# A scheduled attention and FFN kernel: more room behind each wait in the order, measured lengths in the planner, and small softmax steps moved

## The chip, the cores and the metric

The kernel runs on one core of a Trainium2 chip. The metric is the device time of one execution in microseconds. PE is the matrix engine (TensorE), PEld its weight loads, ACT is ScalarE, DVE is VectorE, POOL is GpSimd, and SP is the engine that issues the DMA transfers. Each of them runs its own instructions in the order in which they were written, and waits for semaphores of the others.

## The reference, cut to what matters

```python
def mab(q, kv):                       # scale = 1/sqrt(128)
    s = scale * (q @ kv.T)
    a = exp(s - s.max(-1));  a /= a.sum(-1) + 1e-09
    return a @ kv
h = mab(I, x)                         # x: 4 x 12480 x 128, I: 32 x 128
y = mab(x, h)                         # 4 x 12480 x 128
out = relu(y @ w_in) ** 2 @ w_out     # w_in: 128 x 2048, w_out: 2048 x 128
```

All is float32. The first attention has 32 queries over all tokens of a batch; the second has each token as a query over 32 keys.

## The kernel before, in words

A batch is cut into 13 units of 960 tokens, so there are 52 units, and a unit is two blocks of 480 tokens. After a start-up (the first attention of batch 0, and the weights), units run one after the other. For each unit PE does the FFN: 32 products named `h` of 480 columns (line 755) give relu inputs in PSUM, and 96 products named `op` (line 795) multiply the squared relus by `w_out`. Two `h` products fill one of two PSUM buffers, called a pair here: `h_4_0_2` is pair 2 of block 0 of unit 4 (order rows leave the batch out, and end in a running number). ACT empties a pair with a relu (line 763, into `g`), and after two pairs it squares `g` in place (line 774). DVE rounds `g` to `hi` (line 778) and takes the rest `lo` = `g` - `hi` (line 782); PE multiplies `hi` by two parts of `w_out` and `lo` by one. The buffers: two for `h`, three for `g`, two for `hi`, two for `lo`.

Beside this FFN stream every unit carries small work for later units: transposes of x (`xtp`, copied to `xt`), the two attentions' scores (`na`) and mixes (`nb`), and the second attention's softmax: a maximum, the difference `d`, its exponential on ACT, the rounded part `sk` and its rest, the sum `z`, and three small steps on 120x8 elements (lines 637, 640, 644: add 1e-9, invert, square) that give `zz`. `zz` scales the output when a block is turned back (`otp`, line 823, into `osb`). `ot` is the copy of a finished `op` sum out of PSUM, and `sw` that of the attention weights, which DMAs then spread into `st`, the input of `h`. In batch 3 there is no first attention left to do, so its units carry less.

The order on every engine comes from a list scheduler, class `Plan`, when the program is built. A task has an engine (or two to choose from, `"ACT|DVE"`), a length in ns, a due time, and tasks that it needs. `offer` sets when it is ready: the latest end of what it needs, plus a latency by the engine that it waits for. `room_at` adds 60 ns after the last user of a buffer. At each step `run` takes for each engine the task that can start first, by due time among those ready at once, and of these the earliest. `port` keeps GpSimd tasks and some VectorE tasks from overlapping in the plan. The chip then runs the orders as written, whatever times the plan had in mind.

Of the kernel before, what the change touches and what calls it, by code (L numbers as in the profile page):

```python
# [21 lines left out]
TS = 120  # L22
# [5 lines left out]
class Task:  # L28
    def __init__(self, engine, ns, fn, due, needs, port, mode, takes, order):
        self.engine, self.ns, self.fn, self.due = engine, ns, fn, due  # L30
        self.needs, self.port, self.mode, self.takes, self.order = needs, port, mode, takes, order
        self.start = self.end = self.ready = None
        self.waiting = 0
        self.then = []
# [9 lines left out]
class Plan:  # L44
# [7 lines left out]
    LATENCY = {"PE": 220.0, "ACT": 150.0, "DVE": 150.0, "POOL": 150.0, "SP": 2500.0}  # L52
    SWITCH = 95.0

    def __init__(self, room):
        self.room, self.tasks = room, []

    def add(self, engine, ns, fn, due, needs=(), port=False, mode=None, takes=(), reads=()):

        t = Task(engine.split("|"), ns, fn, due, [n for n in needs if n is not None], port, mode, takes, len(self.tasks))  # L60
        for b in list(takes) + list(reads):
            b.users.append(t)
        self.tasks.append(t)
        return t

    def run(self):
# [20 lines left out]
        def room_at(t):  # L87
            at = 0.0
            n = {}
            for b in t.takes:  # L90
                n[b.tag] = n.get(b.tag, 0) + 1
                old = taken.get(b.tag, [])
                i = len(old) + n[b.tag] - 1 - self.room[b.tag]
                if i >= 0:
                    for u in (old[i].users if i < len(old) else ()):
                        if u.end is None:
                            return None
                        at = max(at, u.end + 60.0)
            return at
# [42 lines left out]
def induced_attention_then_squared_relu_ffn(  # L142
# [22 lines left out]
    XT, OT, ST, SKH = ("ACT|DVE", "ACT|DVE"), ("ACT|DVE", "ACT|DVE"), "ACT|DVE", "ACT|DVE"  # L165
# [11 lines left out]
    plan = Plan(dict(xn=3, early=6, xt=NU + 1, m=2, h=2, o=2, g=GB, hi=HB, lo=LB, st=2, sw=2, words=2))  # L177
# [57 lines left out]
    def weights(name, load, use, due):  # L235
# [54 lines left out]
        t = add("SP", 2100, words, due - 6000, takes=[buf])  # L290
# [65 lines left out]
    class First:  # L356
        def __init__(self, b, u, due, early=False):

            self.b, self.u, self.early, self.n = b, u, early, f"{b}_{u}"
            self.s = s = state.setdefault(b, {"xt": {}, "chain": None, "bxt": {}})  # L360
            self.bx = Buffer("early" if early else "xn")
            self.bt = s["bxt"][u] = Buffer("xt")
            lead = 2500 if early else 8000

            def load():
                self.xn = (pools["early"] if early else xn_pool).tile(
                    [TS, NT, C], F32, tag="xn", name=f"xn_{self.n}"
                )
                nc.sync.dma_start(self.xn, x_v[b, :, u * NT:(u + 1) * NT, :])

            loaded = add("SP", 2000, load, due - lead - (4000 if early else 20000), takes=[self.bx])
            self.turned = []
            for k in range(2):
                self.turned.append(self.turn(k, due - lead + k * lead * 0.4, loaded))

        def turn(self, k, due, loaded):
# [18 lines left out]
            t = add("PE", 420, turn, due, [loaded] + self.turned,  # L395
# [194 lines left out]
    class Second:  # L590
# [13 lines left out]
        def weigh(self, scored, where, bank_, due, step):  # L604
# [31 lines left out]
            def norm1():  # L636
                nc.vector.tensor_scalar_add(v["z"], v["z"], 1e-9)

            def norm2():
                nc.vector.reciprocal(v["z"], v["z"])  # L640

            def norm3():
                s["zz", u] = tiny.tile([TS, G, 1], F32, tag="zz", name=f"zz_{n}")
                nc.vector.tensor_mul(s["zz", u], v["z"], v["z"])


            def high():
                v["sk"] = att.tile([TS, Q, 2, 2, M], F32R, tag="sk", name=f"sk_{n}")
                copy(th, v["sk"][:, :, :, 0, :], v["d"].rearrange("t (k q) m -> t q k m", q=Q))
# [39 lines left out]
            th = add(SKH, (300, 250), high, d + 3 * step, [tp], port=True)  # L689
# [44 lines left out]
    def ffn_block(b, u, k, second, t0, first_needs):  # L734
# [7 lines left out]
        def quad(j, last):  # L742
# [4 lines left out]
            for i in range(2):  # L747
# [19 lines left out]
                t = add("PE", 217, lambda wide=wide: wide(0), d, need, takes=[bh], reads=[second.bst])  # L767
                w.setdefault("begun", t)
                t = add("PE", 217, lambda wide=wide: wide(1), d, [t], reads=[bh, second.bst])
                relus.append(add("ACT", 855, relu, d + 1000, [t] + first_needs + relus,  # L770
# [13 lines left out]
            sq = add("ACT", 1696, square, due + 4000, relus, reads=[bg])  # L784
            th = add("DVE", 1070, high, due + 5700, [sq], port=True, takes=[bhi], reads=[bg])
            tl = add("DVE", 2076, low, due + 7800, [th], port=True, takes=[blo], reads=[bg, bhi])
            for m, (wo, name, from_, buf) in enumerate((
                (wo_hi, "hi", th, bhi), (wo_lo, "hi", th, bhi), (wo_hi, "lo", tl, blo),
            )):
                for i in range(2):  # L790
# [10 lines left out]
                    last = add("PE", 434, products, due + 8000 + 600 * (2 * m + i), [from_, last, w_outs[j]],  # L801
# [32 lines left out]
        td = add(OT[k], (455, 570), done, end + 1000, [last], reads=[bo])  # L834
# [77 lines left out]
```

## Time and profile before

| | us |
|---|---|
| median of three runs (lowest to highest) | 1776.12 (1775.27 to 1777.15) |
| the profiled execution's own time | 1777.57 |
| its span, first to last instruction | 1775.8 |
| busy: PE / PEld / ACT / DVE / POOL | 1736.6 / 1415.7 / 1652.7 / 1641.0 / 22.2 |

The profiled execution is one run, taken by the hardware profiler; its time is 1.8 us above its span and 1.45 us above the median. Busy is the union of an engine's instructions. A matmul's record is longer than the step to the next one, since they overlap: 480 columns are 0.38 us in a record and 0.22 us from start to start. So PE reads as busy even where it lost time, and its losses are seen in the starts.

### The profile page before, as it was taken

What the parts mean: (1) busy time and instruction counts of PE and PEld (TensorE: products, weight loads), DVE (VectorE), ACT (ScalarE), POOL (GpSimd) and SP (SyncE); (2) the same over time, 40 slices, a digit from 0 to 9 for tenths busy, and PEclk for the clock granted to TensorE, in tenths of its full rate; (3) what the DMA queues carried; (4) which work ended last, traced back from release to release, by engine and by line L of the source; (5) the groups of instructions that cost most, each with busy time, mean ns of one, the idle gap of its engine ahead of it and who ended that gap; (6) DMA issues with size and microseconds to landing.
All of it is one profiled execution on the core that took longest, in us unless ns stands there. A gap on an engine that the chain in (4) does not pass through costs nothing.

```text
span 1775.8 us, 24582 instructions
## 1 busy us (share of the span) xinstructions
PE 1736.6 (98%) x9625; PEld 1415.7 (80%) x9625; DVE 1641.0 (92%) x1736; ACT 1652.7 (93%) x1765; POOL 22.2 (1%) x22
## 2 busy tenths in 40 slices
PE   7799999999999999999999999999999999999998
PEld 4488888888788888888888888888887788888886
DVE  6799999999999999999999999999999998999988
ACT  6699999999999999999999999999999999999997
POOL 1200000000000000000000000000000000000000
PEclk9899999999999999999999999999999999999999
DMA  9211211211121211211211211111101001010110
GB/s 234 62 45 45 56 34 45 56 35 44 34 56 45 56 37 43 56 45 36 59 29 45 56 45 38 52 46 48 31 23 42 26 23 45 23 45 23 35 33 23
DMA packets 33532, 82.48 MB, mean 46 GB/s; under 512 B 5032, under 2 KB 20424, under 8 KB 33416
## 3 DMA queue, kind: packets, MB, share of 16 engines
q1 hardware_dynamic: 33416, 80.91, 17.4%
q8 instruction: 76, 1.25, 0.3%
q14 instruction: 40, 0.33, 0.1%
HBM read 29.77 MB, written 25.56 MB: 31 GB/s over the span
## 4 chain that ended last, share of the span: by engine, by line
PE 67%; ACT 20%; issue 9%; DVE 2%; DMA 1%; SPq 0%; ACTq 0%; DVEq 0%
PE op L795 43%; PE h L755 15%; ACT g L763 13%; ACT g L774 6%; PE otp L815 2%; PE xtp L388 1%; PE ap L660 1%; PE na L599 1%; DMA xn<-in_x_dram 1%; PE wp L559 1%; PE s2t L616 1%; PE na L403 1%; DVE lo L782 1%; PE ep L437 1%; ACT xt L224 1%
## 5 line engine op out<-in xcount | busy, mean ns | idle before, releaser
L782 DVE TENSOR_TENSOR lo<-g,hi 128x1920 fp32r<-128x1920 f32 x416 | 895.6, 2153 | 13.0 <-DVE hi L778 0.9
L763 ACT ACTIVATE g<-h 128x960 f32<-128x960 f32 x832 | 783.0, 982 | 47.8 <-PE h L755 42.1
L774 ACT ACTIVATE g<-g 128x1920 f32<-128x1920 f32 x416 | 759.4, 1826 | 5.1
L755 PE MATMUL h<-st,hw 128*128 128x480 f32 x1664 | 644.3, 388 | 15.4 <-ACT g L763 12.5
L778 DVE CAST hi<-g 128x1920 fp32r<-128x1920 f32 x416 | 480.1, 1154 | 78.8 <-ACT g L774 75.3
L795 PE MATMUL op<-lo,wo_hi 128*128 128x480 f32 x1664 | 511.1, 389 | 0.3 <-DVE lo L782 0.3
L795 PE MATMUL op<-hi,wo_lo 128*128 128x480 f32 x1664 | 506.0, 390 | 0.0
L795 PE MATMUL op<-hi,wo_hi 128*128 128x480 f32 x1664 | 481.8, 382 | 0.2 <-DVE hi L778 0.2
L755 PEld LDWEIGHTS h<-st,hw 128*128 128x128 f32 x1664 | 314.3, 189 | 108.3 <-ACT g L763 55.7
L795 PEld LDWEIGHTS op<-hi,wo_hi 128*128 128x128 f32 x1664 | 311.4, 188 | 50.3 <-DVE hi L778 0.9
L795 PEld LDWEIGHTS op<-hi,wo_lo 128*128 128x128 f32 x1664 | 299.6, 188 | 50.6 <-issue 11.7
L795 PEld LDWEIGHTS op<-lo,wo_hi 128*128 128x128 f32 x1664 | 302.2, 189 | 40.4 <-issue 2.7
L224 ACT COPY ot<-op 128x480 f32<-128x480 f32 x99 | 55.8, 564 | 27.1 <-PE op L795 26.9
L823 DVE TENSOR_TENSOR osb<-otp,zz 120x512 f32<-120x512 f32 x104 | 71.2, 684 | 4.2 <-PE otp L815 2.5
L388 PE MATMUL xtp<-ident,xn 120*128 120x120 f32 x416 | 62.7, 278 | 7.3 <-DMA xn<-in_x_dram 5.4
L388 PEld LDWEIGHTS xtp<-ident,xn 120*128 120x128 f32 x416 | 51.0, 147 | 21.0 <-issue 6.2
L815 PE MATMUL otp<-ident,ot 128*120 128x128 f32 x416 | 62.4, 272 | 0.6 <-ACT ot L224 0.6
L815 PEld LDWEIGHTS otp<-ident,ot 128*120 128x120 f32 x416 | 48.9, 137 | 15.6 <-ACT ot L224 6.6
L224 ACT COPY xt<-xtp 128x480 f32<-128x480 f32 x66 | 36.3, 555 | 13.7 <-PE xtp L388 13.6
L660 PEld LDWEIGHTS ap<-identr,sk 120*128 120x128 f32 x208 | 31.5, 193 | 4.8 <-DVE hw L568 1.5
L599 PE MATMUL na<-xt,hT 128*32 128x240 f32 x416 | 32.3, 382 | 0.0
L660 PE MATMUL ap<-identr,sk 120*128 120x120 f32 x208 | 29.5, 265 | 0.0
(95 smaller groups left out, 673.9 us busy)
## 6 DMA issues: line engine op xcount, KB each, us to landing
xn<-in_x_dram SPq DMA_DIRECT2D x52, 480.0 KB, 4.3
st<-sw SPq DMA_DIRECT2D x208, 120.0 KB, 2.6
out_dram<-osb SPq DMA_DIRECT2D x52, 480.0 KB, 3.5
words_i<-in_moe_w_in_dram SPq DMA_DIRECT2D x4, 512.0 KB, 10.3
words_o<-in_moe_w_out_dram SPq DMA_DIRECT2D x4, 512.0 KB, 7.5
ind_sb<-in_inducing_dram SPq DMA_DIRECT2D x1, 16.0 KB, 1.8
```

Of the source, the lines that this page charges most:

```text
L224: ENG[task.by](dst, src)
L388: nc.tensor.transpose(v["tp"][:, t * TS:(t + 1) * TS], self.xn[:, 4 * k + t, :], ident[:TS, :TS])
L599: nc.tensor.matmul(where[q * M:(q + 1) * M, :], self.s["hT"][:, :M], self.s["xt"][self.u][:, q * 2 * TS:(q + 1) * 2 * TS], start=True, sto ...
L660: nc.tensor.matmul(ap[:, q * TS:(q + 1) * TS], v["sk"][:, q].rearrange("t k a m -> t (k a m)"), identr[:TS, :TS], start=(q == 0), stop=(q ...
L755: nc.tensor.matmul(c["hp"][:, l, :BLK], s["hw"][:, f * P:(f + 1) * P], s["st", u][:, k, :], start=True, stop=True,)
L763: nc.scalar.activation(v["g"][:, 2 * i:2 * i + 2, :], c["hp"][:, :, :BLK], AF.Relu)
L774: nc.scalar.activation(v["g"], v["g"], AF.Square)
L778: nc.vector.tensor_copy(v["hi"], v["g"])
L782: nc.vector.tensor_sub(v["lo"], v["g"], v["hi"])
L795: nc.tensor.matmul(w["op"][:, :BLK], wo[:, 4 * j + l, :], v[name][:, l, :], start=(j == m == l == 0), stop=(j == NQ - 1 and m == 2 and l = ...
L815: nc.tensor.transpose(tp[:TS, q * P:(q + 1) * P], w["ot"][:, q * TS:(q + 1) * TS], ident)
L823: nc.vector.tensor_mul(s["osb", u].rearrange("t (q k) c -> t k q c", k=2)[:, k], w["tp"][:TS, :].rearrange("t (q c) -> t q c", q=Q), s["zz ...
```

## The change

The planner gets three edits. A task now has a margin `late`, added to the latency behind everything that it waits for: 200 ns for PE and 100 ns for the others in the main part, none in the start-up, and some set by hand. A PE task that waits for a PE task has no latency at all (before: 220 ns). A buffer is free 100 ns plus the margin after its last user (before: 60 ns). Some lengths and the latency behind DVE are new numbers. In the second attention the add of 1e-9 goes to GpSimd; then GpSimd squares, and DVE inverts the square; the copy to `sk` is always on DVE.

```diff
-    LATENCY = {"PE": 220.0, "ACT": 150.0, "DVE": 150.0, "POOL": 150.0, "SP": 2500.0}
+    LATENCY = {"PE": 220.0, "ACT": 150.0, "DVE": 185.0, "POOL": 150.0, "SP": 2500.0}
+    LATE = {"PE": 200.0, "other": 100.0}
...
+        if late is None:
+            late = self.LATE["PE" if engine == "PE" else "other"] if due > self.begin else 0.0
...
-            t.ready = max([n.end + self.LATENCY[n.by] for n in t.needs], default=0.0)
+            t.ready = 0.0
+            for n in t.needs:
+                own = n.by == "PE" and t.engine == ["PE"]
+                t.ready = max(t.ready, n.end + (0.0 if own else self.LATENCY[n.by] + t.late))
...
-                        at = max(at, u.end + 60.0)
+                        at = max(at, u.end + 100.0 + t.late)
...
+    LATE_G1, LATE_OT = 150.0, 400.0
...
             def norm1():
-                nc.vector.tensor_scalar_add(v["z"], v["z"], 1e-9)
+                nc.gpsimd.tensor_scalar(v["z"], v["z"], 1e-9, 0.0, ALU.add, ALU.add)
             def norm2():
-                nc.vector.reciprocal(v["z"], v["z"])
+                v["zz"] = tiny.tile([TS, G, 1], F32, tag="z3", name=f"z3_{n}")
+                nc.gpsimd.tensor_mul(v["zz"], v["z"], v["z"])
             def norm3():
                 s["zz", u] = tiny.tile([TS, G, 1], F32, tag="zz", name=f"zz_{n}")
-                nc.vector.tensor_mul(s["zz", u], v["z"], v["z"])
+                nc.vector.reciprocal(s["zz", u], v["zz"])
...
-            t = add("DVE", 75, norm1, d + 5 * step, [t])
-            t = add("DVE", 113, norm2, d + 5 * step, [t])
-            self.zz = add("DVE", 198, norm3, d + 5 * step, [t])
+            t = add("POOL", 150, norm1, d + 5 * step, [t])
+            t = add("POOL", 150, norm2, d + 5 * step, [t])
+            self.zz = add("DVE", 120, norm3, d + 6 * step, [t])
...
-                t = add("PE", 217, lambda wide=wide: wide(0), d, need, takes=[bh], reads=[second.bst])
+                t = add("PE", 219, lambda wide=wide: wide(0), d, need, takes=[bh], reads=[second.bst], late=LATE_G1)
...
-            sq = add("ACT", 1696, square, due + 4000, relus, reads=[bg])
-            th = add("DVE", 1070, high, due + 5700, [sq], port=True, takes=[bhi], reads=[bg])
+            sq = add("ACT", 1706, square, due + 4000, relus, reads=[bg], late=0)
+            th = add("DVE", 1070, high, due + 5700, [sq], port=True, late=200, takes=[bhi], reads=[bg])
...
-        td = add(OT[k], (455, 570), done, end + 1000, [last], reads=[bo])
+        td = add(OT[k], (455, 570), done, end + 1500, [last], reads=[bo], late=LATE_OT)
```

What that does to the orders is seen at three places. First PE in batch 1, where unit 4 begins. Before, the two halves of a pair stand apart, with `op` products between them, and ten products stand between the end of pair 2 and pair 4, which takes the same PSUM buffer:

```order
L755 MATMUL h_4_0_2_6272<-st_4_6103,hw_4764 128x480
L795 MATMUL op_3_1_6184<-hi_3_1_2_6251,wo_hi 128x480 x2
L755 MATMUL h_4_0_2_6272<-st_4_6103,hw_4764 128x480
L795 MATMUL op_3_1_6184<-hi_3_1_2_6251,wo_hi 128x480 x2
L755 MATMUL h_4_0_3_6284<-st_4_6103,hw_4764 128x480
L795 MATMUL op_3_1_6184<-hi_3_1_2_6251,wo_lo 128x480 x2
L755 MATMUL h_4_0_3_6284<-st_4_6103,hw_4764 128x480
L795 MATMUL op_3_1_6184<-hi_3_1_2_6251,wo_lo 128x480 x2
L795 MATMUL op_3_1_6184<-lo_3_1_2_6255,wo_hi 128x480 x2
L755 MATMUL h_4_0_4_6297<-st_4_6103,hw_4764 128x480
```

The same pairs in the changed order:

```order
L770 MATMUL h_4_0_2_6282<-st_4_6137,hw_4761 128x480
L810 MATMUL op_3_1_6199<-hi_3_1_3_6274,wo_hi 128x480 x2
L770 MATMUL h_4_0_2_6282<-st_4_6137,hw_4761 128x480
L810 MATMUL op_3_1_6199<-hi_3_1_3_6274,wo_hi 128x480 x2
L810 MATMUL op_3_1_6199<-hi_3_1_3_6274,wo_lo 128x480 x4
L770 MATMUL h_4_0_3_6298<-st_4_6137,hw_4761 128x480 x2
L613 MATMUL na_5_6303<-xt_5_2070,hT_4759 32x240 x4
L417 MATMUL na_5_6303<-xt_5_6102,indT 32x240 x4
L471 MATMUL nb_4_6312<-xn_4_5368,et_4_6061 32x128 x8
L810 MATMUL op_3_1_6199<-lo_3_1_3_6284,wo_hi 128x480 x4
L810 MATMUL op_4_0_6331<-hi_4_0_0_6301,wo_hi 128x480 x2
L770 MATMUL h_4_0_4_6334<-st_4_6137,hw_4761 128x480 x2
```

The halves of pairs 3 and 4 now stand together (so they do for 681 of the 832 pairs of the kernel, for one before), and 14 products of 480 columns and the whole group `na`, `nb` stand between the end of pair 2 and pair 4.

Second ACT, whose relus free those buffers, in the same stretch. Before, pair 0's relu stands ahead of the last square of the block before, pair 1's behind it:

```order
L763 ACTIVATE g_4_0_0_6253<-h_4_0_0_6225 128x960
L774 ACTIVATE g_3_1_3_6211<-g_3_1_3_6211 128x1920
L763 ACTIVATE g_4_0_0_6253<-h_4_0_1_6262 128x960
L774 ACTIVATE g_4_0_0_6253<-g_4_0_0_6253 128x1920
L763 ACTIVATE g_4_0_1_6291<-h_4_0_2_6272 128x960
```

Now that square stands ahead of both:

```order
L789 ACTIVATE g_3_1_3_6242<-g_3_1_3_6242 128x1920
L778 ACTIVATE g_4_0_0_6270<-h_4_0_0_6251 128x960
L778 ACTIVATE g_4_0_0_6270<-h_4_0_1_6272 128x960
L789 ACTIVATE g_4_0_0_6270<-g_4_0_0_6270 128x1920
L778 ACTIVATE g_4_0_1_6296<-h_4_0_2_6282 128x960
```

Third DVE in unit 10 of batch 1, where the softmax of unit 11 ends. Before, the sum `z`, the add and the reciprocal stood there on DVE alone:

```order
L634 TENSOR_REDUCE z_1_11_8251<-d_11_8208 120x8
L637 TENSOR_SCALAR z_1_11_8251<-z_1_11_8251 120x8
L224 CAST sw_11_8257<-ap_11_8246 128x480
L778 CAST hi_10_0_2_8265<-g_10_0_2_8167 128x1920
L640 RECIPROCAL z_1_11_8251<-z_1_11_8251 120x8
L782 TENSOR_TENSOR lo_10_0_2_8281<-g_10_0_2_8167,hi_10_0_2_8265 128x1920
L644 TENSOR_TENSOR zz_11_8294<-z_1_11_8251 120x8
```

In the changed order two GpSimd steps run somewhere between these rows, and the reciprocal waits for them:

```order
L648 TENSOR_REDUCE z_1_11_8292<-d_11_8260 120x8
L797 TENSOR_TENSOR lo_10_0_2_8295<-g_10_0_2_8211,hi_10_0_2_8268 128x1920
L793 CAST hi_10_0_3_8321<-g_10_0_3_8264 128x1920
L238 COPY xt_12_8323<-xtp_12_0_8324 128x480
L659 RECIPROCAL zz_11_8342<-z_1_11_8334 120x8
L797 TENSOR_TENSOR lo_10_0_3_8344<-g_10_0_3_8264,hi_10_0_3_8321 128x1920
```

In batch 3 the rows between are `hi`, `lo`, `hi`. Over the kernel the copies of 128x480 elements on DVE go from 78 to 120 (`ot` 5 to 53, `xt` 38 to 52, `sw` 35 to 15), and fall on ACT by as many; `sk` on DVE goes from 6 to 52, its 46 others leave ACT.

## Rows read from the trace of the kernel before

**Rows 1.** The page: span, and busy us (share) x instructions by engine.
```profile
span 1775.8 us, 24582 instructions
PE 1736.6 (98%) x9625; PEld 1415.7 (80%) x9625; DVE 1641.0 (92%) x1736; ACT 1652.7 (93%) x1765; POOL 22.2 (1%) x22
```

**Rows 2.** Busy by window: PE, PEld, DVE, ACT, POOL (instructions); PEclk, DMA share, GB/s.
```profile
570.00:934.00 364.00, 361.29 (x2010) 298.10 (x2009) 342.88 (x362) 345.15 (x367) 2.21 (x1) 1.00 0.17 44
1364.00:1739.00 375.00, 370.61 (x1794) 303.98 (x1793) 347.26 (x312) 360.31 (x348) 0.00 (x0) 1.00 0.12 32
```

**Rows 3.** Waits, whole run: who waited for whom, us in total, times, longest.
```profile
DVE hi L778 <- ACT g L774: 75.3, 93, 1.3
PEld h L755 <- ACT g L763: 55.7, 142, 1.2
ACT g L763 <- PE h L755: 42.1, 128, 0.7
```

**Rows 4.** Timeline of PE, batch 1: start, length, what [idle before].
```profile
634.53 0.60 PE L795 MATMUL op<-hi,wo_lo 128*128 128x480 f32 x2
635.19 0.60 PE L795 MATMUL op<-hi,wo_lo 128*128 128x480 f32 x2
635.63 0.60 PE L795 MATMUL op<-lo,wo_hi 128*128 128x480 f32 x2
636.48 0.49 PE L755 MATMUL h<-st,hw 128*128 128x480 f32 x1 [0.24 <-ACT g L763]
636.80 0.59 PE L795 MATMUL op<-lo,wo_hi 128*128 128x480 f32 x2
```

**Rows 5.** Timeline of ACT, the same stretch.
```profile
633.76 1.81 ACT L774 ACTIVATE g<-g 128x1920 f32<-128x1920 f32 x1
635.48 1.81 ACT L763 ACTIVATE g<-h 128x960 f32<-128x960 f32 x2
```

**Rows 6.** Timeline of PE, the unit before, its one other loss.
```profile
618.15 0.48 PE L755 MATMUL h<-st,hw 128*128 128x480 f32 x1
618.47 0.59 PE L795 MATMUL op<-lo,wo_hi 128*128 128x480 f32 x2
```

**Rows 7.** Timeline of PE, unit 4 of batch 3, its two losses.
```profile
1500.64 1.04 PE L795 MATMUL op<-hi,wo_lo 128*128 128x480 f32 x4
1501.95 0.49 PE L755 MATMUL h<-st,hw 128*128 128x480 f32 x1 [0.27 <-ACT g L763]
1502.28 0.60 PE L795 MATMUL op<-lo,wo_hi 128*128 128x480 f32 x2
...
1506.01 0.60 PE L795 MATMUL op<-lo,wo_hi 128*128 128x480 f32 x2
...
1507.04 0.59 PE L795 MATMUL op<-lo,wo_hi 128*128 128x480 f32 x2
```

**Rows 8.** Groups by line: instructions, x count | busy us, mean ns | idle before.
```profile
L224 ACT COPY ot<-op 128x480 f32<-128x480 f32 x99 | 55.8, 564 | 27.1 <-PE op L795 26.9
L224 DVE COPY xt<-xtp 128x480 f32<-128x480 f32 x38 | 24.7, 651 | 0.4 <-PE xtp L388 0.4
L224 ACT CAST sk<-d 120x256 fp32r<-120x256 f32 x46 | 18.8, 408 | 1.4
L224 DVE CAST sk<-d 120x256 fp32r<-120x256 f32 x6 | 1.7, 287 | 0.0
L637 DVE TENSOR_SCALAR z<-z 120x8 f32<-120x8 f32 x52 | 8.7, 168 | 1.1
```

**Rows 9.** Timelines of POOL and DVE, where the two meet or don't.
```profile
37.24 1.23 DVE L479 SCALAR_TENSOR_TENSOR zs<-zs,fade,z 128x1 f32<-128x1 f32 x1
463.24 0.22 DVE L479 SCALAR_TENSOR_TENSOR zs<-zs,fade,z 128x1 f32<-128x1 f32 x1
463.63 2.20 POOL L537 TENSOR_SCALAR sums<-ones,zs 128x128 f32<-128x128 f32 x1 [390.33 <-PE h L755]
1313.94 0.38 POOL L537 TENSOR_SCALAR sums<-ones,zs 128x128 f32<-128x128 f32 x1 [418.10 <-DVE zs L479]
```

More of the change, by code (lines that the diff above doesn't have):

```diff
@@ L28, with __init__ @@
 class Task:
-    def __init__(self, engine, ns, fn, due, needs, port, mode, takes, order):
+    def __init__(self, engine, ns, fn, due, needs, port, mode, takes, late, order):
         self.engine, self.ns, self.fn, self.due = engine, ns, fn, due
-        self.needs, self.port, self.mode, self.takes, self.order = needs, port, mode, takes, order
+        self.needs, self.port, self.mode, self.takes = needs, port, mode, takes
+        self.late, self.order = late, order
         self.start = self.end = self.ready = None
@@ L50, with __init__, add @@
     ENGINES = ("PE", "ACT", "DVE", "POOL", "SP")
-    LATENCY = {"PE": 220.0, "ACT": 150.0, "DVE": 150.0, "POOL": 150.0, "SP": 2500.0}
+    LATENCY = {"PE": 220.0, "ACT": 150.0, "DVE": 185.0, "POOL": 150.0, "SP": 2500.0}
     SWITCH = 95.0
[L55 to L60, printed above, removed]
+    LATE = {"PE": 200.0, "other": 100.0}
+    def __init__(self, room, begin):
+        self.room, self.begin, self.tasks = room, begin, []
+    def add(self, engine, ns, fn, due, needs=(), port=False, mode=None, takes=(), reads=(), late=None):
+        if late is None:
+            late = self.LATE["PE" if engine == "PE" else "other"] if due > self.begin else 0.0
+        needs = [n for n in needs if n is not None]
+        t = Task(engine.split("|"), ns, fn, due, needs, port, mode, takes, late, len(self.tasks))
         for b in list(takes) + list(reads):
@@ L176, in induced_attention_then_squared_relu_ffn @@
     ps_m = ctx.enter_context(tc.tile_pool(name="ps_m", bufs=2, space=PSUM))
-    plan = Plan(dict(xn=3, early=6, xt=NU + 1, m=2, h=2, o=2, g=GB, hi=HB, lo=LB, st=2, sw=2, words=2))
+    plan = Plan(dict(xn=3, early=6, xt=NU + 1, m=2, h=2, o=2, g=GB, hi=HB, lo=LB, st=2, sw=2, words=2), T_MAIN)
     def bank(name):
@@ L289, in weights @@
         kw = dict(reads=[buf])
-        t = add("SP", 2100, words, due - 6000, takes=[buf])
+        t = add("SP", 2100, words, due - 6000, takes=[buf], late=0)
         t = add("DVE", 340, clamp, due, [t], port=True, **kw)
@@ L369, in load @@
                 nc.sync.dma_start(self.xn, x_v[b, :, u * NT:(u + 1) * NT, :])
-            loaded = add("SP", 2000, load, due - lead - (4000 if early else 20000), takes=[self.bx])
+            loaded = add("SP", 2000, load, due - lead - (4000 if early else 20000), takes=[self.bx], late=0)
             self.turned = []
@@ L766, in quad @@
                 need = [second.ready, s["wide"][j]]
-                t = add("PE", 217, lambda wide=wide: wide(0), d, need, takes=[bh], reads=[second.bst])
+                t = add("PE", 219, lambda wide=wide: wide(0), d, need, takes=[bh], reads=[second.bst], late=LATE_G1)
                 w.setdefault("begun", t)
-                t = add("PE", 217, lambda wide=wide: wide(1), d, [t], reads=[bh, second.bst])
-                relus.append(add("ACT", 855, relu, d + 1000, [t] + first_needs + relus,
+                t = add("PE", 219, lambda wide=wide: wide(1), d, [t], reads=[bh, second.bst])
+                relus.append(add("ACT", 864, relu, d + 1000, [t] + first_needs + relus, late=0,
                                  takes=[bg] if i == 0 else [], reads=[bh] + ([bg] if i else [])))
@@ L782, in low @@
                 nc.vector.tensor_sub(v["lo"], v["g"], v["hi"])
-            sq = add("ACT", 1696, square, due + 4000, relus, reads=[bg])
-            th = add("DVE", 1070, high, due + 5700, [sq], port=True, takes=[bhi], reads=[bg])
-            tl = add("DVE", 2076, low, due + 7800, [th], port=True, takes=[blo], reads=[bg, bhi])
+            sq = add("ACT", 1706, square, due + 4000, relus, reads=[bg], late=0)
+            th = add("DVE", 1070, high, due + 5700, [sq], port=True, late=200, takes=[bhi], reads=[bg])
+            tl = add("DVE", 2070, low, due + 7800, [th], port=True, late=0, takes=[blo], reads=[bg, bhi])
             for m, (wo, name, from_, buf) in enumerate((
```

10 lines of the change are left out of this document (5 added, 5 removed).

## The prediction, made before the changed kernel ran

> **What bounds the kernel now.** I read the page's totals first. PE is busy for 1736.6 of 1775.8 us, ACT for 93% and DVE for 92% [rows 1], so three engines are nearly full. The table by windows says the same of the steady stages: in batch 1 PE is busy 361.3 of 364 us, DVE 342.9, ACT 345.2; in batch 3 PE 370.6 of 375, ACT 360.3, DVE 347.3. PE has its full clock in both [rows 2]. Then the table of waits, to see which engines still wait. DVE waits 75.3 us for the squares, ACT 42.1 us for `h`, and the weight loads of `h` 55.7 us in 142 places for the relu that empties their PSUM buffer [rows 3]. The first two are slack of engines that are not the bound. The third is on PE, which is the bound. But that number is idle time of the load queue, which runs ahead of the matmuls, so it is not yet PE's loss.
>
> The loss is in the starts. In an undisturbed stretch three products take 0.66 us from start to start, 0.22 each (634.53 to 635.19, with an `h` between) [rows 4]. One us later the same three take 1.17 us (635.63 to 636.80): the `h` among them starts at 636.48 only, when ACT's relu is done. That costs 0.51 us. The unit has one other loss, where `h` at 618.15 is followed at 618.47 instead of 0.22 later: 0.10 us [rows 6]. In batch 3, five products take 1.64 us (1500.64 to 1502.28) instead of 1.10, and three take 1.03 (1506.01 to 1507.04) instead of 0.66 [rows 7]: 0.54 and 0.37, together 0.91. These places recur at the same point of nearly every unit.
>
> Why does it wait? ACT does a square of 1.81 us from 633.76, and the relu that empties the buffer can begin only behind it, at 635.48; it ends some 0.9 us later, at 636.4 [rows 5]. ACT in turn starts its relus late where the second half of a pair comes late, 128 times [rows 3]. So a margin in the plan that is too thin for the chip, halves of pairs that stand apart, and a square between two relus make PE late together.
>
> **The sum, part by part.** All of it is against the profiled execution (1777.6 us, span 1775.8); the median is 1.45 us lower.
>
> *What can be won.* 39 units of batches 0 to 2 at 0.61 us and 13 of batch 3 at 0.91 us are 23.8 + 11.8 = 35.6 us. This is a ceiling: the change removes no instruction from PE, and PE's other time is the products themselves.
>
> *The place in batches 0 to 2.* In the old order ten products, 2.2 us, stand between pair 2's end and pair 4, which needs pair 2's buffer. In the new one 14 products stand there, 3.1 us, and the group `na`, `nb`, which I leave out of the count. On ACT's side pair 2's relu comes behind pair 1's relu and a square: 0.9 + 1.81 + 0.9 = 3.6 us from pair 1's arrival on (two relus took 1.81 us [rows 5]). Pair 2 arrives at least 0.9 us behind pair 1 (its two halves and two products between), so its relu is done at most 2.7 us after pair 2, against 3.1 us and `na`, `nb` on PE. The wait goes, with 0.4 us to spare and more. I count all 23.8 us less 1 for units where it is closer.
>
> *The places in batch 3.* The first (0.54 us) goes: in the new order the relu of that buffer stands ahead of the square. At the second (0.37) the square stands ahead of the relu in both orders; counting steps of 0.22, 0.9 and 1.81 us I find PE and ACT there within 0.1 to 0.3 us of each other. I take it as kept: 13 x 0.37 = 4.8 us not won. Bounds: all kept (0 of 11.8 us won) or all won.
>
> *Copies that change engine.* 42 more copies of 128x480 on DVE at 0.651 us are +27 us there, and 46 of `sk` at 0.287 are +13; GpSimd takes two small steps of about 0.168 from DVE, 52 times each: -17 us [rows 8]. So DVE gets about 23 us more, ACT 42 x 0.564 + 46 x 0.408 = 42 us less. DVE's 1641 us become 1664. It must then fit into a shorter span: in batch 1 it goes from 342.9 of 364 us to some 348, while 364 less 11 units' gain of 0.6 leaves 357. There is room, but only 0.8 us a unit. I take 0 for the copies as long as that room holds.
>
> *The two GpSimd steps.* The trace has none of 120x8. The nearest are `sums` of 128x128, 0.38 us where DVE leaves it alone (1313.94), and 2.20 us where a `lo` of DVE is running (463.63); and the other way round a DVE step of 0.22 us that takes 1.23 while GpSimd adds weights [rows 9]. So the two engines exclude each other in some instructions. The reciprocal stands three big DVE instructions behind the sum `z`: in 33 units one of them is a copy from PSUM of 0.65 us, in which both steps may fit; in batch 3 they are `hi`, `lo`, `hi`, so the steps fit only where DVE idles before a `hi`. If they miss, the reciprocal holds DVE: two steps at 0.38 and some 0.2 of hand-over, 0.9 us. Bounds per unit: 0 (hidden) and 0.9 (all of it on PE), 0 to 49 us. `zz` itself is needed only by `osb` later. Queued behind the reciprocal is a `lo` or a `hi`, for which PE's `op` waits; today DVE is ahead of PE often enough to idle 75.3 us before `hi`, and that idle time covers a late step. I take 0.08 us a unit, 4 us, near the lower end, because the nearest rows for cover (DVE idle some 0.8 us at 93 places) are of the size of the delay.
>
> One rule speaks against this part. Rows 9 show GpSimd blocked until a two-input DVE instruction ends, and DVE blocked by GpSimd. The Trainium skill, page "SBUF — State Buffer", section "Who interferes with whom", says why: GpSimd shares one pair of SBUF ports with VectorE, held for a whole instruction, and a VectorE instruction with two SBUF inputs or in a 2-port mode is shut out by it, and shuts it out. By that rule `hi`, `lo` and the low part of `sk` all collide with the new steps, whereas a copy from PSUM does not; the trace agrees in 2.20 against 0.38 us. What it would do here is the third rival below.
>
> *Start-up and end.* The start-up's orders are nearly the same, since the margin is zero there; DVE loses two small steps and gains the `sk` copy, and GpSimd's two steps stand ahead of the last weights. I take 0, with 2 us either way. The last unit is ordered alike.
>
> Sum: 35.6 - 1 - 4.8 - 4 = 26 us won. 1777.6 - 26 = 1751.6 for a run like the profiled one, 1750 on the median.
>
> **The rivals.**
>
> *Everything is won.* The second place in batch 3 goes too and GpSimd hides: 1776 - 35.6 = 1740.5. For it: the planner now counts on later semaphores than the trace shows, so its order should run early on the chip. Against: ACT and PE are within 0.3 us at that place.
>
> *The wait moves to VectorE.* DVE has 23 us more work and a shorter span, and what room is left, 0.8 us a unit, goes into GpSimd's collisions. PE then waits for `hi` and `lo`, of which rows 3 have none. If 0.5 us a unit reaches PE on half the units, 13 us are lost beside the 4 already counted: 1750 + 13 = 1763; if 0.3 us more on the rest, 1771. For it: DVE at 95%. Against: it idles 75.3 us now.
>
> *GpSimd's steps hold VectorE, and the kernel is slower.* A step that comes while `lo` runs waits for its end, as `sums` did; the next `hi` follows at once, so the second step waits again; the reciprocal holds DVE for both, and `lo` behind it makes PE wait. If 0.9 us a unit reaches PE, 52 x 0.9 = 47 us stand against 30 won: 1776 - 30 + 47 = 1793. The kernel is slower from 0.6 us a unit on. Against: DVE's idle time, and the copy from PSUM in 33 of the 52 units.
>
> *The order changes and nothing is won.* The waits turn up at other pairs: 1773 to 1779. Against: the largest place has 0.4 us to spare and more, and the first of batch 3 has lost its square.
>
> **How the numbers follow.** Chances: the forecast 0.43 (its own range 1745 to 1757), everything won 0.22, VectorE 0.18, GpSimd 0.11, nothing won 0.06. The likeliest is 1750. The range from 1738 (everything won, and 2 us of start-up) to 1770 (nearly all of the VectorE case) holds some 0.8. A difference under 0.2%, 3.6 us, can hardly be told from none. Faster by more: 0.43 + 0.22 + 0.18 = 0.83; within: 0.06; slower: 0.11.
>
> **What would show it.** Right: the wait of `h` loads for `g` falls from 55.7 us to under 20, and a unit's period (from one place to the same one in the next unit) shrinks by some 0.6 us in batches 0 to 2 and 0.5 in batch 3. The second place in batch 3 shows as a late `h` in every unit. The GpSimd steps show as POOL records of up to 0.4 us, or over 1 us where they meet a `lo`, and the reciprocal as a DVE wait for POOL, a few tenths in each unit. The forecast is wrong if PE's `op` waits for `hi` or `lo` by tens of us, or if DVE's wait for POOL is above 25 us with PE late behind it.

## The result, and the profile after

The changed kernel takes 1753.54 us (median of four runs, 1752.45 to 1754.27) against 1776.34 for the one before: a ratio of 0.9871, 95% interval 0.9854 to 0.9889, or 22.8 us won. Its profiled execution took 1754.27 us with a span of 1752.5, where the one before had 1777.57 and 1775.8; the parts below are taken between these two spans, 23.35 us apart.

The page's totals answer to [rows 1], and the table by windows to [rows 2] (here about 11 units of batch 1 and 12 of batch 3, nearly the same stretches of work). Columns of the windows: length, busy time of PE, PEld, DVE, ACT, POOL with instructions, PE's clock, DMA share, GB/s.

```profile
span 1752.5 us, 24391 instructions
PE 1724.4 (98%) x9625; PEld 1418.5 (81%) x9625; DVE 1666.2 (95%) x1720; ACT 1635.2 (93%) x1677; POOL 148.5 (8%) x126
```

```profile
570.00:922.00 352.00, 352.00 (x1980) 293.91 (x1979) 340.63 (x355) 335.83 (x343) 26.52 (x23) 1.00 0.19 47
1340.00:1705.00 365.00, 365.00 (x1793) 301.87 (x1792) 354.17 (x311) 351.97 (x324) 36.66 (x24) 1.00 0.13 33
```

PE's records leave no gap in either stretch any more, at full clock. DVE is at 340.6 of 352 us and 354.2 of 365: about 1 us a unit is left there. The waits of the whole run answer to [rows 3]; columns: us in total, times, longest.

```profile
DVE hi L793 <- ACT g L789: 22.3, 56, 1.1
PEld h L770 <- ACT g L778: 17.4, 74, 0.9
...
PEld op L810 <- DVE lo L797: 6.6, 21, 0.7
```

The loads of `h` wait 17.4 us for the relu's `g` instead of 55.7, and in their place a small wait for DVE's `lo` has come up. The stretch of [rows 4, 5], in the same unit of batch 1, now reads so, on PE first (start, length, what):

```profile
635.54 0.60 PE L770 MATMUL h<-st,hw 128*128 128x480 f32 x2
635.98 0.60 PE L810 MATMUL op<-hi,wo_hi 128*128 128x480 f32 x2
```

and on ACT:

```profile
630.34 1.81 ACT L789 ACTIVATE g<-g 128x1920 f32<-128x1920 f32 x1
632.05 1.81 ACT L778 ACTIVATE g<-h 128x960 f32<-128x960 f32 x2
```

Both halves of a pair come together, two products in 0.44 us (635.54 to 635.98). ACT still does a square between its relus, but the two that begin at 632.05, of pairs 2 and 3, are done at 633.9, well ahead of pair 4 at 635.54, which takes pair 2's buffer: no row of this stretch has an idle time.

**Where the 23.35 us come from.** The first `h` of a unit serves as a mark. First the marks of before, for units 0, 4, 6, 40 and 51 (start, length, what):

```profile
71.68 0.74 PE L755 MATMUL h<-st,hw 128*128 128x480 f32 x1 [1.43 <-DMA st<-sw]
198.19 0.38 PE L755 MATMUL h<-st,hw 128*128 128x480 f32 x1
263.92 0.38 PE L755 MATMUL h<-st,hw 128*128 128x480 f32 x1
1387.20 0.38 PE L755 MATMUL h<-st,hw 128*128 128x480 f32 x1
1730.71 0.38 PE L755 MATMUL h<-st,hw 128*128 128x480 f32 x1
```

and the same units after the change:

```profile
74.87 0.74 PE L770 MATMUL h<-st,hw 128*128 128x480 f32 x1 [1.66 <-DMA st<-sw]
202.42 0.38 PE L770 MATMUL h<-st,hw 128*128 128x480 f32 x1
267.00 0.38 PE L770 MATMUL h<-st,hw 128*128 128x480 f32 x1
1373.43 0.38 PE L770 MATMUL h<-st,hw 128*128 128x480 f32 x1
1709.21 0.38 PE L770 MATMUL h<-st,hw 128*128 128x480 f32 x1
```

A unit of batch 0 falls from (263.92 - 198.19) / 2 = 32.87 us to (267.00 - 202.42) / 2 = 32.29, by 0.58; a unit of batch 3 from (1730.71 - 1387.20) / 11 = 31.23 to (1709.21 - 1373.43) / 11 = 30.53, by 0.70. From the first `h` to the last unit's it is 1659.03 us before and 1634.34 after: 24.7 won. The start-up before the first `h` lost 3.2 us (71.68 to 74.87), and the last unit won 1.85 (45.09 to 43.24 us to the end of the span). 24.7 + 1.85 - 3.2 = 23.35.

### The profile page after: what moved, and what is told of

Read it like the earlier page. It is cut to its first block, busy times and chain, and to the rows that moved or that the text cites. A ratio compares the mean times of both kernels' runs of the same rounds, so it can differ in the third digit from the quotient of the medians.

```text
span 1752.5 us, 24391 instructions
## 1 busy us (share of the span) xinstructions
PE 1724.4 (98%) x9625; PEld 1418.5 (81%) x9625; DVE 1666.2 (95%) x1720; ACT 1635.2 (93%) x1677; POOL 148.5 (8%) x126
## 4 chain that ended last, share of the span: by engine, by line
PE 95%; DMA 2%; DVE 1%; ACT 1%; issue 0%; SPq 0%; ACTq 0%; DVEq 0%
PE op L810 63%; PE h L770 21%; PE otp L830 3%; PE xtp L402 2%; PE na L613 2%; DMA words_i<-in_moe_w_in_dram 1%; PE ap L675 1%; PE nb L471 1%; PE wp L573 1%; PE na L417 1%; PE s2t L630 1%; PE ep L451 1%; DMA words_o<-in_moe_w_out_dram 0%; ACT g L778 0%; PE hp L471 0%
## 5 line engine op out<-in xcount | busy, mean ns | idle before, releaser
L770 PE MATMUL h<-st,hw 128*128 128x480 f32 x1664 | 520.5, 386 | 2.5 <-DMA st<-sw 1.7
L793 DVE CAST hi<-g 128x1920 fp32r<-128x1920 f32 x416 | 479.4, 1152 | 23.8 <-ACT g L789 22.3
L810 PE MATMUL op<-lo,wo_hi 128*128 128x480 f32 x1664 | 471.1, 394 | 0.5 <-DVE lo L797 0.5
L810 PE MATMUL op<-hi,wo_lo 128*128 128x480 f32 x1664 | 431.7, 380 | 0.0
L770 PEld LDWEIGHTS h<-st,hw 128*128 128x128 f32 x1664 | 306.9, 188 | 65.8 <-ACT g L778 17.4
L810 PEld LDWEIGHTS op<-hi,wo_lo 128*128 128x128 f32 x1664 | 311.8, 188 | 50.9
L810 PEld LDWEIGHTS op<-lo,wo_hi 128*128 128x128 f32 x1664 | 292.9, 188 | 53.4 <-issue 11.8
L651 POOL TENSOR_SCALAR z<-z 120x8 f32<-120x8 f32 x52 | 89.6, 1723 | 1478.1 <-DVE z L648 1478.1
L238 ACT COPY xt<-xtp 128x480 f32<-128x480 f32 x52 | 28.8, 559 | 14.3 <-PE xtp L402 13.6
L655 POOL TENSOR_TENSOR z<-z 120x8 f32<-120x8 f32 x52 | 37.7, 724 | 4.3
L238 DVE COPY ot<-op 128x480 f32<-128x480 f32 x53 | 34.5, 651 | 0.0
```

What stands on the lines that cost most here:

```text
L238: ENG[task.by](dst, src)
L651: nc.gpsimd.tensor_scalar(v["z"], v["z"], 1e-9, 0.0, ALU.add, ALU.add)
L770: nc.tensor.matmul(c["hp"][:, l, :BLK], s["hw"][:, f * P:(f + 1) * P], s["st", u][:, k, :], start=True, stop=True,)
L793: nc.vector.tensor_copy(v["hi"], v["g"])
L810: nc.tensor.matmul(w["op"][:, :BLK], wo[:, 4 * j + l, :], v[name][:, l, :], start=(j == m == l == 0), stop=(j == NQ - 1 and m == 2 and l = ...
```

## The experiments

Each was timed beside runs of the kernel before on one chip; those had a median of 1776.25 us for e1 to e4, 1777.63 for e5 to e8 and 1777.22 for e9 to e12. So kernels of different groups are compared by their ratios.

**e1, the pairs alone.** The kernel before, with PE's delay behind itself taken out:

```diff
-            t.ready = max([n.end + self.LATENCY[n.by] for n in t.needs], default=0.0)
+            t.ready = 0.0
+            for n in t.needs:
+                own = n.by == "PE" and t.engine == ["PE"]
+                t.ready = max(t.ready, n.end + (0.0 if own else self.LATENCY[n.by]))
```

> The kernel before, with one part of the change: a matmul counts no delay behind another matmul of PE, so that the two halves of an h pair stand together. Theory 'pairs': most of the 22.8 us comes from this (halves that stand apart make the relu late, and the relu makes the next h late): 1753 to 1762 us, and the weight loads of h wait for g well under 30 us (55.7 before, 17.4 after). Theory 'margins': the order only runs safely with the later places: 1770 to 1779 us, the wait of h loads above 40 us. Theory 'engines': ACT is relieved by the copies that moved, nothing here: 1773 to 1779 us.

1754.97 us, ratio 0.9877 (0.9862 to 0.9892): 21.3 us with three lines. The loads of `h` wait for `g` 15.3 us in 55 places (55.7 in 142 before). In its trace 699 of the 832 pairs stand together; before it was five, all of unit 0 (not one, as said above). The edit also takes the 220 ns from between the `op` products of one sum, so what it is worth is not the halves alone: no run parts the two.

**e2, the engine moves alone.** The kernel before, with the `norm` steps on GpSimd and `sk` on DVE as the change has them, nothing else:

```diff
...
-            t = add("DVE", 75, norm1, d + 5 * step, [t])
-            t = add("DVE", 113, norm2, d + 5 * step, [t])
-            self.zz = add("DVE", 198, norm3, d + 5 * step, [t])
+            t = add("POOL", 150, norm1, d + 5 * step, [t])
+            t = add("POOL", 150, norm2, d + 5 * step, [t])
+            self.zz = add("DVE", 120, norm3, d + 6 * step, [t])
...
-            th = add(SKH, (300, 250), high, d + 3 * step, [tp], port=True)
+            th = add("DVE", 210, high, d + 3 * step, [tp], port=True)
```

> The kernel before, with the engine moves alone: two small steps of the normalization on GpSimd, the high part of sk always on DVE; the planner's latencies and lengths as before. Theories 'pairs' and 'margins': 1773 to 1780 us, no gain, since the pairs stand apart as before. Theory 'engines': 1753 to 1762 us. Rival that GpSimd's steps cost something which the order hides in the whole change: 1780 us or more, with DVE's reciprocal waiting for POOL.

1779.67 us, ratio 1.0020 (1.0011 to 1.0029): no gain, a loss of 3.4 us. The loads of `h` still wait 50.7 us. The profiled span is only 0.9 us above that of before, so the trace doesn't say where the rest goes.

**e3, no late places.** The change with its margins taken out:

```diff
-    LATE = {"PE": 200.0, "other": 100.0}
+    LATE = {"PE": 0.0, "other": 0.0}
...
-                        at = max(at, u.end + 100.0 + t.late)
+                        at = max(at, u.end + 60.0 + t.late)
```

and the named ones and DVE's latency likewise.

> The changed kernel with every late place taken out (LATE 0, the named ones 0, the room of buffers 60 ns as before, DVE's latency 150 as before); pairs stand together, the engine moves stay. Theory 'pairs': 1753 to 1760 us, as the change or a few us more, the wait of h loads under 30 us. Theory 'margins': 1768 us or more, and PE waits for DVE's hi or lo and for the relu in every unit.

1764.23 us, ratio 0.9930 (0.9917 to 0.9942): neither theory's time. The wait of the `h` loads is gone as in the change; what is left, in the table of PE's load queue, is another one:

```profile
PEld h L770 <- ACT g L778: 15.8, 59, 1.0
PEld op L810 <- DVE lo L797: 12.1, 46, 0.8
PEld op L810 <- DVE hi L793: 11.9, 62, 0.6
```

The weight loads wait 24 us for DVE's `hi` and `lo`, against 8.4 with the margins (6.6 for `lo`, 1.8 for `hi`). So the margins pay on VectorE's side. In e1, which has no margins either but leaves the steps on their old engines, it is 14.4 (10.5 and 3.9), and e1 is 9.3 us faster. That looks like a price of the moved work, but most of it lies elsewhere: with the first `h` at 75.70 instead of 72.06 and a unit 0 of 31.91 us instead of 30.06, 5.5 of the 8.7 us between the two spans are lost before unit 1 begins. Against the change it is 2.9 of 9.9 us (first `h` at 74.87, unit 0 29.85).

**e4, no engine moves.** The change with the `norm` steps on DVE and `sk` on either engine as before (the diff of e2, reversed).

> The changed kernel with the engine moves taken back: the normalization's three steps on DVE as before (lengths 75, 113, 198), sk's high part on ACT or DVE as the planner chooses; the pairs and the late places stay. Theories 'pairs' and 'margins': 1750 to 1757 us, no difference above 3 us. Theory 'engines': 1765 us or more. Rival that GpSimd's steps cost time: 1745 to 1750 us, faster than the change.

1753.99 us, ratio 0.9875 (0.9862 to 0.9889): the same as the change. Beside the margins these two moves neither win nor cost. The `ot` copies, which the planner moves by itself under the other edits, stay on DVE (51 of them; 53 in the change, 5 before), so this run doesn't price them.

**e5, no pairs, the crude way.** The change with PE treated as any other engine:

```diff
-                own = n.by == "PE" and t.engine == ["PE"]
+                own = False
```

> The changed kernel with one part taken back: a matmul again counts 220 ns and the late place behind another matmul of PE, so that the halves of the pairs should stand apart; the late places elsewhere, the lengths and the engine moves stay. Theory 'pairs' (the first run alone won 21.3 of 22.8 us with it): 1768 to 1780 us, the wait of h loads for g above 40 us. Rival that the late places reach the same by another way: 1752 to 1760 us.

1915.03 us, ratio 1.0769 (1.0753 to 1.0785), far outside both. This edit does more than the one that it was to undo: each `op` of a sum needs the one before, so the planner now counts 220 + 200 ns between any two of them and stretches every unit (35.25 us). It shows that a margin must not stand between instructions of one in-order engine, and says nothing on the pairs.

**e9, no pairs, the clean way.** The change with PE's old 220 ns behind itself and no margin on top of it:

```diff
-                t.ready = max(t.ready, n.end + (0.0 if own else self.LATENCY[n.by] + t.late))
+                t.ready = max(t.ready, n.end + self.LATENCY[n.by] + (0.0 if own else t.late))
```

> The changed kernel with PE behind PE by 220 ns as before and without a late place on top; late places elsewhere, lengths and engine moves stay. So it is the change less the pairs. Theory 'pairs': 1766 to 1780 us, units of 32.8 us in batches 0 to 2, h loads waiting above 40 us for g. Rival that late places alone do it as well: 1752 to 1757 us, since the relus then come early enough for halves that stand apart.

1767.67 us, ratio 0.9946 (0.9933 to 0.9958). The loads of `h` wait 39.7 us for `g` in 125 places, between the 55.7 of before and the 17.4 of the change. PE's zero delay, and the pairs with it, is worth 13 us beside everything else of the change (0.9946 against 0.9871) and 21.3 without it; the rest alone wins 9.6 us. Both theories hold in part, and their gains overlap. The units show how: only 14 pairs stand together, and in batches 0 and 2 a unit takes 32.8 us as before, but in batch 1 the first `h` of units 16 and 24 are

```profile
597.59 0.49 PE L770 MATMUL h<-st,hw 128*128 128x480 f32 x1
856.14 0.48 PE L770 MATMUL h<-st,hw 128*128 128x480 f32 x1
```

or 32.32 us a unit, as in the change (594.10 and 852.49 there, 32.30). So halves that stand apart need not cost anything; why the order is that good in batch 1 alone was not tried.

**e10, half the margins.** 100 and 50 instead of 200 and 100, the named ones 75, 200 and 100, the room 80.

> The changed kernel with every late place halved (200 and 100 become 100 and 50, the named ones 75, 200 and 100, the room 80). Without any the time was 1764.2, with all 1753.5. If the gain grows evenly with the size: 1757 to 1760 us. If a small margin already gives the order that the chip keeps: 1751 to 1756 us.

1754.49 us, ratio 0.9877 (0.9864 to 0.9891): the whole gain. Half of the margins is enough here; smaller ones were not tried.

**e6, the normalization on DVE.** The change with the three `norm` steps as they were before, `sk` stays on DVE.

> The changed kernel with the three steps of the normalization on DVE again (75, 113 and 198 ns in the plan), all else as changed. Theory that GpSimd's steps are hidden: 1751 to 1756 us, within 3 us of the change, though GpSimd's steps meet DVE's hi and lo there (1.72 and 0.72 us each). Rival that they hold VectorE and cost PE time: 1744 to 1750 us. Rival that DVE at 95% has no room for them: 1757 us or more.

1752.41 us, ratio 0.9861 (0.9844 to 0.9877) against 0.9871 for the change: the same. Its span is 1.5 us shorter, half of that from the start-up (first `h` at 74.14 instead of 74.87). The planner orders every engine anew here (712 pairs together instead of 681, 22 `xt` copies on DVE instead of 52), so this isn't the price of GpSimd's steps alone; by this run they cost some 1 us, or nothing.

**e11, GpSimd's steps doubled.** Behind the two steps, in the same task, two more of the same forms:

```diff
                 nc.gpsimd.tensor_mul(v["zz"], v["z"], v["z"])
+                nc.gpsimd.tensor_scalar(v["z"], v["z"], 1.0, 0.0, ALU.mult, ALU.add)
+                nc.gpsimd.tensor_mul(v["zz"], v["z"], v["z"])
```

> The changed kernel with GpSimd's part of the normalization doubled: behind the two steps the same two forms again (a multiply by one, the product again), in one task, so that the order on every other engine stays. It prices what a GpSimd step costs there. Forecast's term of 0.08 us a unit for two steps: 1757 us or more. Theory that they are hidden and DVE doesn't wait: 1752 to 1755.5 us, DVE's wait for POOL under 3 us. Rival that each collision holds VectorE: 1765 us or more.

1761.11 us, ratio 0.9913 (0.9899 to 0.9926): 0.0042 above the change, or 7.5 us, though the first two steps had cost little or nothing. The orders of the other engines stay. Its waits, and the marks of units 4, 6, 40 and 51:

```profile
DVE zz L661 <- POOL z L657: 17.2, 47, 0.4
```

```profile
203.59 0.38 PE L772 MATMUL h<-st,hw 128*128 128x480 f32 x1
268.62 0.38 PE L772 MATMUL h<-st,hw 128*128 128x480 f32 x1
1381.09 0.38 PE L772 MATMUL h<-st,hw 128*128 128x480 f32 x1
1717.12 0.38 PE L772 MATMUL h<-st,hw 128*128 128x480 f32 x1
```

Two units of batch 0 take 65.03 us instead of 64.58; eleven of batch 3 take 336.03 instead of 335.78. DVE waits in 47 units, but in batches 0 to 2 only one unit of two gets longer: unit 4 takes 31.89 us instead of 31.41, unit 5 33.14 as against 33.17, and so on in turn. In such a unit the timeline of its POOL, then DVE, then PE shows how it reaches PE:

```profile
680.72 2.21 POOL L656 TENSOR_SCALAR z<-z 120x8 f32<-120x8 f32 x1
```

```profile
680.74 2.15 DVE L799 TENSOR_TENSOR lo<-g,hi 128x1920 fp32r<-128x1920 f32 x1
683.25 0.20 DVE L661 RECIPROCAL zz<-z 120x8 f32<-120x8 f32 x1 [0.37 <-POOL z L657]
```

```profile
687.17 1.12 PE L812 MATMUL op<-lo,wo_hi 128*128 128x480 f32 x4 [0.19 <-DVE lo L799]
```

The third step came 0.02 us before a `lo` and ended with it, the reciprocal waited 0.37 us, the `hi` and `lo` queued behind it came later, and PE's `op` waits for that `lo`.

**e7, the start-up as before.** The change, with every step due before the main part planned by the old rules (PE behind PE 220, DVE 150, room 60), and the early turns of x without their new order. That order is an edit of the change which the diff ahead of the prediction leaves out: a turn (the transposes `xtp`) now also needs the turn before it, and counts 440 ns instead of 420.

```diff
-                own = n.by == "PE" and t.engine == ["PE"]
+                own = n.by == "PE" and t.engine == ["PE"] and t.due > self.begin
...
-            t = state["turn"] = add("PE", 440, turn, due, [loaded, state.get("turn")] + self.turned,
+            t = state["turn"] = add("PE", 420 if self.early else 440, turn, due, [loaded, None if self.early else state.get("turn")] + self.turned,
```

> The changed kernel, but every step due before the main part is planned as before: PE behind PE by 220 ns, DVE's latency 150, the room of buffers 60 ns, the early turns 420 ns and without the wait for the unit before. So the start-up has the order of before. Theory 'start-up': the first h comes at 71.5 to 72.5 us again (71.68 before, 74.87 after) and the gain stays to the end: 1749 to 1751 us. Rival that what the start-up loses is slack that the first units give back anyway: 1752.5 to 1754.5 us.

1751.88 us, ratio 0.9853 (0.9838 to 0.9867). The first `h` comes at 70.35 us, the span is 1748.1 (1752.5 for the change), and the units behind are nearly the same: what the start-up lost was lost to the end. How much that is stays open. The first `h` and the span of the two traces say 4.5 and 4.4 us, but e7's trace has the shortest span of its four runs (1748.1 to 1750.4) and the change's the longest of its four (1750.6 to 1752.5). The ratios say 3.2, with intervals that overlap.

**e8, only the early turns' order taken back.**

> The changed kernel with one edit of the start-up taken back: an early turn of x doesn't wait for the turns of the unit before; the latencies there stay as changed. If that wait is what the start-up loses, the first h comes at 72 us and the time is 1749 to 1751 us; if the latencies (PE behind PE at nothing, DVE 185) reorder the start-up, the first h stays at 74 to 75 us and the time within 1 us of the change.

1753.62 us, ratio 0.9864 (0.9849 to 0.9878). The first `h` is at 73.31, between the two expected marks, and the time doesn't differ from the change's beyond the noise. It is not shown that the loss has two parts which add up: e10 keeps the order of the turns, PE's zero delay and DVE's 185 ns, its rules for the start-up differ from the change's only in the room of 80 instead of 100 ns, and its first `h` comes at 72.10. Each of these marks is one trace. So no single rule is shown to make the loss.

**e12, e7 and e6 together.**

> The changed kernel with the start-up planned as before (that run had a ratio of 0.9853 against 0.9871) and the normalization's steps on DVE (0.9861): the two undone parts together. If the start-up is all that is to be won: ratio 0.985 to 0.9855, some 1750 us where before takes 1776.3. If the steps on GpSimd cost their 1 us as well: 1748 to 1749.5 us. Rival that the steady order differs and eats it: 1752 us or more.

1750.44 us, ratio 0.9852 (0.9838 to 0.9865): the best number of the study, first `h` at 71.40, span 1748.9. It doesn't differ from e7, so of these two parts only the start-up shows a gain.

## Why the prediction was right, step by step

*The wait on PE.* It was the loss, and it went: the loads' wait fell from 55.7 us to 17.4 (under 20 was predicted), and the period by 0.58 us in batch 0 (0.61 less GpSimd's 0.08) and 0.70 in batch 3 (0.54 less 0.08). What the prediction left open was which edit does it. e1 shows that PE's zero delay, with the pairs together, does most of it, e9 that the rest does a part of it without them, in batch 1 all of it.

*The sum.* To the first `h` of unit 40, 39 units of batches 0 to 2 and one of batch 3, the gain is (1387.20 - 71.68) - (1373.43 - 74.87) = 17.0 us; 23.8 - 1 - 3.1 = 19.7 were counted for the 39, 0.51 each, and 0.46 for the one. Regular units give a little more, 0.58 each. The rest is lost in units that the count took as regular: unit 0 goes from 28.76 to 29.85 us (PE's granted clock from 75 to 80 us is 0.50 of full speed, 0.92 before), and the four units around the first change of batch win 1.0 us together (428.23 to 562.61 before, 427.56 to 560.93 after) instead of 2.0. Why this change of batch wins less was not tried. The eleven units behind give 343.51 - 335.78 = 7.7 us, 0.70 each where 0.46 was counted. So the total is near the forecast in part by luck: units before batch 3 and the start-up gave less than was counted, batch 3 and the end more.

*The second place in batch 3*, taken as kept at 0.37 us, is gone, and a smaller one has come up at another pair. Before, the late `h` there was the first half of pair 5 of block 1. In unit 5 of batch 3 that pair now comes on time, 0.88 us behind the start of four `op` products, and takes 0.44:

```profile
1518.17 1.04 PE L810 MATMUL op<-lo,wo_hi 128*128 128x480 f32 x4
1519.05 0.60 PE L770 MATMUL h<-st,hw 128*128 128x480 f32 x2
1519.49 1.02 PE L810 MATMUL op<-hi,wo_hi 128*128 128x480 f32 x4
```

But at the start of block 1 four halves of `h`, of the last pair of block 0 and the first of block 1, take 1510.74 - 1509.61 = 1.13 us instead of 0.88:

```profile
1509.61 1.29 PE L770 MATMUL h<-st,hw 128*128 128x480 f32 x4
1510.74 0.59 PE L810 MATMUL op<-lo,wo_hi 128*128 128x480 f32 x2
```

and here ACT's square stands ahead of the relus that PE waits for:

```profile
1507.49 1.80 ACT L789 ACTIVATE g<-g 128x1920 f32<-128x1920 f32 x1
1509.19 2.88 ACT L778 ACTIVATE g<-h 128x960 f32<-128x960 f32 x3
```

That recurs in the units of batch 3 at the same place: 0.25 us a unit instead of 0.37, about half of the surplus there (0.70 against 0.46). The late `h` in every unit, which was named as a sign, is seen, but not for the reason given: the size is right by luck.

*Copies that change engine* were taken as nothing. The work is what was counted (compare [rows 8]): DVE is busy for 25 us more where 23 were worked out, with 53 `ot` copies of 651 ns on it. For `sk`, and for most of the `xt` copies (18 on DVE in e4, 52 in the change), e4 shows that they cost nothing beside the margins. The `ot` copies stay on DVE in e4 too, so for them it is not shown.

*GpSimd's two steps.* They were charged 4 us; by e6 it is about 1 or nothing. The collision itself is as foreseen, and its records are longer than the rows that I had, 1723 ns in the mean for the first step:

```profile
L651 POOL TENSOR_SCALAR z<-z 120x8 f32<-120x8 f32 x52 | 89.6, 1723 | 1478.1 <-DVE z L648 1478.1
```

But the reciprocal, group L659, idles 0.1 us in the whole run, where a few tenths in each unit were foretold. One unit of batch 1 shows why, DVE first, then POOL:

```profile
707.86 0.41 DVE L648 TENSOR_REDUCE z<-d 120x8 f32<-120x256 f32 x1
708.18 2.15 DVE L797 TENSOR_TENSOR lo<-g,hi 128x1920 fp32r<-128x1920 f32 x1
710.25 1.16 DVE L793 CAST hi<-g 128x1920 fp32r<-128x1920 f32 x1
711.32 0.65 DVE L238 COPY xt<-xtp 128x480 f32<-128x480 f32 x1
711.89 0.20 DVE L659 RECIPROCAL zz<-z 120x8 f32<-120x8 f32 x1
```

```profile
708.36 3.09 POOL L651 TENSOR_SCALAR z<-z 120x8 f32<-120x8 f32 x1 [31.82 <-DVE z L648]
711.53 0.20 POOL L655 TENSOR_TENSOR z<-z 120x8 f32<-120x8 f32 x1
```

The first step is shut out by `lo` and by the `hi` that follows it at once, 3.09 us, and ends at 711.45, 0.04 us after that `hi`; the second takes 0.20 us under the copy from PSUM; the reciprocal follows 0.16 us later. So the cover was not DVE's idle time, as the prediction argued (its wait for the squares fell from 75.3 to 22.3 us), but the instructions that the order puts between `z` and the reciprocal. That holds in batch 3 as well, where they are `hi`, `lo`, `hi` and the prediction had the steps fit only into idle time: the first ends 0.10 us after the `hi`, the second with the `lo`, and the last `hi` covers the rest. The third rival's mechanism is there, and e11 shows how near: two steps more, and DVE waits up to 0.4 us, and every other unit of batches 0 to 2 takes 0.5 us longer. The Trainium skill, page "SBUF — State Buffer", section "Who interferes with whom", says that an instruction which holds the shared ports blocks the other engine until its end, and that a VectorE instruction with at most one SBUF input, outside the 2-port modes, doesn't contend: the trace agrees, in 3.09 us behind `lo` and `hi` and 0.20 under the copy from PSUM.

*Start-up and end* is the term that was wrong: 0 with 2 us either way was taken, and the start-up lost 3.2 while the end won 1.85. The step that failed is "the start-up's orders are nearly the same, since the margin is zero there": the margin is zero, but PE's delay behind itself, DVE's latency, the buffers' room and the order of the turns changed there too. In the change's trace the place is at 43.8 us. Rows of POOL, DVE, ACT and PE after the change:

```profile
43.84 1.27 POOL L357 TENSOR_TENSOR a_o<-a_o,wo_hi 128x512 f32<-128x512 f32 x1 [6.27 <-ACT wo_hi L353]
45.20 1.32 POOL L358 TENSOR_TENSOR wo_lo<-a_o,b_o 128x512 fp32r<-128x512 f32 x1
```

```profile
43.86 1.54 DVE L268 TENSOR_SCALAR hc_o<-words_o 128x512 f32<-128x512 f32 x1 [0.26 <-DMA words_o<-in_moe_w_out_dram]
45.32 1.21 DVE L436 SCALAR_TENSOR_TENSOR neg<-mx,neg 128x1 f32<-128x1 f32 x1
```

```profile
46.63 0.46 ACT L443 ACTIVATE e<-sp,neg 128x240 f32<-128x240 f32 x1 [2.19 <-DVE neg L436]
```

```profile
47.24 0.68 PE L451 MATMUL ep<-ident,e 128*120 128x128 f32 x2 [2.13 <-ACT e L443]
```

The weights' `hc_o` now stands ahead of `neg`, starts 0.02 us behind a GpSimd instruction and takes 1.54 us instead of 0.41; `neg` meets the next one and takes 1.21 instead of 0.16; ACT's exponential and PE's `ep` wait some 2.2 us for it. In e10 `hc_o` stands ahead of `neg` too, but takes 0.42 us, `neg` behind it 1.28, and PE idles 0.73 us there. So the order alone isn't the loss; how the two meet GpSimd is part of it. PE's clock falls in the same place (last section).

What e7 gains over the change is most of this term. At its real size the start lost 3.2 us and the end won 1.4 (1.85 less the 0.46 that was counted for the last unit). With that the sum would have been 26 - 3.2 + 1.4 = 24.2 us and the forecast 1752; what is left is the balance of the units, above.

## What to carry to other kernels

In a list scheduler, count no delay between instructions of one in-order engine: it can pull apart what belongs together (here 21.3 us in three lines), and a margin added to it is worse still (e5). Margins for late semaphores paid here, where VectorE has little room (10.7 us, e3), and half of them did as well (e10). Price work on an engine that shares a resource by doubling it: a cost of nothing can stand less than 0.2 us from its edge (e11).

## What the hardware did that I had not expected

*PE's clock in the start-up.* The late `ep` may cost more than its 2.1 us. Windows of 45 to 75 us (PE busy, PEld, DVE, ACT, POOL, then PEclk), first the kernel after the change, then before, then e7:

```profile
45.00:75.00 30.00, 19.39 (x95) 9.86 (x91) 21.74 (x46) 11.70 (x28) 9.13 (x10) 0.59 0.25 64
```

```profile
45.00:75.00 30.00, 21.32 (x135) 11.21 (x135) 21.32 (x46) 14.34 (x33) 10.21 (x8) 0.73 0.27 69
```

```profile
45.00:75.00 30.00, 21.60 (x151) 11.14 (x146) 22.22 (x49) 14.22 (x31) 10.23 (x10) 0.77 0.27 68
```

PE's granted clock falls in the idle 2.13 us, is at its lower level, 1.2 GHz, in all of 47.5 to 70 us, and a pair of `ep` takes 0.68 us where it took 0.43 before. Over the 30 us the mean is 0.59 of full speed, against 0.73 before and 0.77 in e7. The other traces go the same way: where this mean is 0.70 or above (before, e1, e2, e7, e10, e12), the first `h` comes at 70.35 to 72.10 us, and where it is 0.64 or below (the change, e3, e4, e6, e8, e9, e11), at 73.31 to 75.70; e5, with 0.66 and 72.25, is between. That the clock, and not the waits that go with it, makes the 3.2 us was not tried by itself.

*GpSimd doesn't get in between two VectorE instructions that overlap.* The 104 records of its small steps come in levels: 0.20 us in 37 of them, 1.08 behind a `hi`, about 2.14 behind a `lo`, and 3.09 behind a `lo` with a `hi` at once behind it, in 18. `lo` ended at 710.33, and the waiting step still lost to the `hi` that had begun at 710.25. Between a `hi` and the `lo` made from it, which starts 0.10 us after the end of `hi`, a step does get in: in the 12 units where these two stand behind `z`, its record ends at the start of `lo` (1358.30 to 1359.38, `hi` done at 1359.28, `lo` from 1359.39).
